# Transposing by the DMA crossbar instead of TensorE: q and the token-mixed rows of batches 1 to 7

## The chip, the cores and the metric

One core of one Trainium2 chip runs the whole program. The metric is the device time of one execution in microseconds, median over several executions. Each run carries the span and the mean clock that the throttle granted to TensorE; a run more than 1.5% above the fastest of the same kernel is called slow, and verdicts use the fast runs alone.

## The reference, cut to what matters

```python
# q, k, v: (8, 8, 576, 64);  out: (8, 576, 512)
k_p, v_p = mean of 8 neighbouring rows of k, v            # 576 -> 72 keys
attn = softmax(q @ k_p.T / 8);  x = attn @ v_p            # heads side by side: (8, 576, 512)
u   = x + (relu(x.T @ w_tok1) @ w_tok2).T                 # token mixing
out = u + relu(u @ w_ch1) @ w_ch2                         # channel MLP, 512 -> 1536 -> 512
```

Two operands must be turned around on the way. The scores need q with the head dimension on the partitions (`qT`), and the channel MLP needs u with the channels on the partitions (`uT`).

## The kernel before

The program is a sequence of *units*. Unit n is the channel MLP of batch n (96 matmuls of 128x512, cut into 48 steps of two), and between its steps stand the pieces of attention and token mixing of batch n+1, at step numbers from a table. TensorE (PE) and GpSimd (POOL) keep the order of the program text.

```python
def load(b):                                   # called in unit n for batch n+2
    kr = raw.tile([SP, H, POOL, D], BF16, name="kr")          # raw: 2 buffers
    vr = raw.tile([SP, H, POOL, D], BF16, name="vr")
    qb = raw.tile([P, HP, BR * D + D], BF16, name="qb")
    nc.vector.memset(qb[:, :, BR * D:], 0.0)                  # zero padding, each batch
    # ... GpSimd issues the casting loads: kr, qb, vr

def qT(hp):                                    # four times for each batch
    def go():
        ps = ps_tr.tile([P, NE, 2, BP], BF16, name="pt")
        for rr in range(NE):
            nc.tensor.transpose(out=ps[:, rr]..., in_=st["qb"][:, hp, rr * P:(rr + 1) * P], identity=ident)
        # copied from PSUM to st["qT"] by ScalarE (VectorE for batch 0)

def uT(c):                                     # four times for each batch, and tails
    def go():
        for kk in range(4):
            nc.tensor.transpose(out=ps[:, kk, :], in_=src[:, kk * P:(kk + 1) * P], identity=ident)
        # copied from PSUM to uT

def unit(n, at):
    if n + 1 < B:
        load(n + 2)
        batches[n + 1][0]()                    # prepare: tiles; GpSimd pools k and v of batch n+1
    for i, _ in enumerate(unit_steps(n, ...)):  # matmuls of the MLP
        # ... the side pieces of step i: kpT, q0.., o/e (scores), av, at, u0.., t0.. (= uT)
```

The softmax here doesn't subtract the row's maximum and nothing guards it: scores larger than these inputs give would overflow.

## Time and profile before

| | before |
|---|---|
| median of the first runs | 307.52 us (307.4 to 308.53) |
| span of the profiled run, mean clock | 305.8 us, 0.996 |
| PE busy | 284.7 us, 93% |
| the first six units, by the start of their first MLP matmul | 34.3, 30.6, 31.9, 30.8, 31.9, 30.8 us |

From the page of the kernel before: the busy time of PE, the clock granted in 40 slices of the span, and the chain of waits that ended last.

```profile
span 305.8 us, 4631 instructions
...
PE 284.7 (93%) x1864; PEld 150.7 (49%) x1900; DVE 157.2 (51%) x316; ACT 102.7 (34%) x181; POOL 135.8 (44%) x120
...
PEclk9999999999999999999999999999999999999998
...
PE 85%; DVE 6%; ACT 3%; DMA 2%; issue 2%; SPq 0%; ACTq 0%
```

PE is the limit. The table by stretches of the same run, one row for a unit, first three units:

```profile
core 0: us, PE busy (x) PEld busy (x) DVE busy (x) ACT busy (x) POOL busy (x), PEclk, DMA share, GB/s
37.18:71.47 34.29, 32.28 (x218) 16.76 (x222) 23.39 (x46) 14.63 (x25) 18.13 (x14) 1.00 0.88 146
71.47:102.08 30.61, 30.15 (x213) 16.43 (x215) 16.81 (x35) 11.15 (x19) 22.29 (x18) 1.00 0.56 92
102.08:133.99 31.91, 31.37 (x218) 17.04 (x222) 17.93 (x37) 11.15 (x19) 19.81 (x15) 1.00 0.54 95
```

The first number after a stretch is its length. PE is idle for about 0.5 us of units 1 and 2. Next, the timeline of PE around one group of q transposes (start, length, line, output and inputs):

```profile
75.09 0.44 PE L217 MATMUL pt<-ident,qb 128*128 128x128 bf16 x5
75.37 0.59 PE L350 MATMUL p_897<-uT,w_ch_86 128*128 128x512 bf16 x2
```

Five transposes are listed with 0.44 us, but the next matmul starts 0.28 us after the first of them; the rest is pipeline. So a group takes 0.28 us of PE's stream. A u group of four takes 0.23 us in the same way.

### The profile page before, as it was taken

The numbers are of one execution on the slowest core, as the hardware profiler recorded it, in microseconds if no ns is written. First come the engines' busy times: TensorE is split into PE (matmuls) and PEld (weight loads), VectorE is DVE, ScalarE is ACT, GpSimd is POOL, SyncE is SP. The second block draws the span as 40 slices with busy tenths as digits, with TensorE's granted clock in tenths as the row PEclk, the third lists the DMA queues.
The fourth block names the chain that finished last, engine by engine and source line by source line (L and its number), as shares of the span: only waits on it lengthen the run. The fifth ranks groups of instructions, "written<-read, shape, count | busy, mean of one in ns | idle before, by whom it ended". The sixth has DMA issues, their size and how long they took to land.

```text
span 305.8 us, 4631 instructions
## 1 busy us (share of the span) xinstructions
PE 284.7 (93%) x1864; PEld 150.7 (49%) x1900; DVE 157.2 (51%) x316; ACT 102.7 (34%) x181; POOL 135.8 (44%) x120
## 2 busy tenths in 40 slices
PE   5687798999999999999999999999999999999993
PEld 2355345445554555445545554455455545444441
DVE  3235657665375537572656266635673567423321
ACT  2154478203810381018301830084008400310300
POOL 8293110996599059913992399995000000000000
PEclk9999999999999999999999999999999999999998
DMA  7999999844772746271836382110121012104023
GB/s 174 194 204 204 203 200 162 140 95 80 119 118 51 141 64 116 52 145 18 140 71 106 58 139 67 46 27 2 34 69 36 0 39 69 36 23 99 16 49 90
DMA packets 26518, 28.27 MB, mean 92 GB/s; under 512 B 4864, under 2 KB 21376, under 8 KB 26496
## 3 DMA queue, kind: packets, MB, share of 16 engines
q0 software_dynamic: 20160, 17.35, 37.0%
q1 hardware_dynamic: 6336, 10.62, 14.1%
q8 instruction: 15, 0.25, 0.3%
q14 instruction: 7, 0.06, 0.1%
HBM read 35.85 MB, written 9.44 MB: 148 GB/s over the span
## 4 chain that ended last, share of the span: by engine, by line
PE 85%; DVE 6%; ACT 3%; DMA 2%; issue 2%; SPq 0%; ACTq 0%
PE pt L217 3%; PE pt L323 3%; DMA qf<-in_q_dram 2%; DVE x L256 1%; DVE kTs_92 L195 1%; PE pt L190 1%; ACT ex L236 1%; DVE kTs_93 L195 1%; PE p_1105 L362 1%; PE p_2921 L362 1%; PE p_3272 L362 1%; PE p_2473 L362 1%; PE p_2878 L362 1%; PE p_1062 L362 1%; PE p_2610 L362 1%
## 5 line engine op out<-in xcount | busy, mean ns | idle before, releaser
L350 PEld LDWEIGHTS <-w_ch_86 128*128 128x128 bf16 x432 | 40.5, 98 | 32.2 <-issue 0.8
L362 PEld LDWEIGHTS <-GT 128*128 128x128 bf16 x432 | 38.7, 98 | 35.9 <-issue 0.5
L104 POOL DMA_DIRECT2D qb<-in_q_dram x7 | 5.4, 777 | 49.9 <-PE pt L217 49.3
L223 ACT COPY qT<-pt 128x640 bf16<-128x640 bf16 x28 | 19.3, 691 | 8.4 <-PE pt L217 7.3
L217 PE MATMUL pt<-ident,qb 128*128 128x128 bf16 x160 | 14.7, 224 | 6.9 <-DVE qT L221 4.7
L246 PEld LDWEIGHTS <-ex 72*128 72x128 bf16 x320 | 15.2, 98 | 11.4 <-DVE x L256 3.3
L217 PEld LDWEIGHTS <-qb 128*128 128x128 bf16 x160 | 11.3, 100 | 17.4 <-issue 10.6
L323 PEld LDWEIGHTS <-u 128*128 128x128 bf16 x128 | 9.7, 98 | 8.6 <-issue 2.0
L325 DVE COPY uT<-pt 128x512 bf16<-128x512 bf16 x28 | 11.8, 421 | 3.5 <-PE pt L323 3.5
L91 POOL DMA_DIRECT2D kr<-in_k_dram x9 | 7.5, 838 | 8.9 <-DVE t_498 L141 8.0
L233 PEld LDWEIGHTS <-kTs_93 128*72 128x72 bf16 x64 | 7.2, 113 | 8.5 <-issue 1.6
L287 PEld LDWEIGHTS <-w_tok_83 128*128 128x128 bf16 x70 | 6.8, 98 | 8.4 <-issue 0.2
L323 PE MATMUL pt<-ident,u 128*128 128x128 bf16 x112 | 10.8, 219 | 0.1
L233 PEld LDWEIGHTS <-kTs_92 128*72 128x72 bf16 x64 | 7.3, 116 | 7.4 <-DVE kTs_92 L195 0.9
L91 POOL DMA_DIRECT2D vr<-in_v_dram x9 | 7.5, 834 | 5.6 <-PE p_396 L390 5.6
L305 PEld LDWEIGHTS <-w_tok_84 128*128 128x128 bf16 x64 | 6.2, 98 | 7.2 <-issue 0.3
L195 DVE COPY kTs_93<-pt 64x576 bf16<-64x576 bf16 (+1 forms) x10 | 4.0, 395 | 4.4 <-PE pt L190 4.3
L190 PEld LDWEIGHTS <-kp 72*128 72x128 bf16 x64 | 3.3, 99 | 4.6 <-DVE kp L208 1.9
L195 DVE COPY kTs_92<-pt 64x576 bf16<-64x576 bf16 (+1 forms) x9 | 3.7, 406 | 3.0 <-PE pt L190 2.0
L190 PE MATMUL pt<-ident,kp 72*128 72x72 bf16 x64 | 3.8, 199 | 1.1 <-DVE kp L208 0.6
L203 PEld LDWEIGHTS <-ident 72*72 72x72 bf16 x32 | 4.3, 135 | 0.7 <-issue 0.2
L355 ACT ACTIVATE GT<-p_3149 128x512 bf16<-128x512 f32 x1 | 0.6, 598 | 11.5 <-PE p_3149 L350 11.5
(806 smaller groups left out, 693.9 us busy)
## 6 DMA issues: line engine op xcount, KB each, us to landing
out_dram<-o SPq DMA_DIRECT2D x72, 128.0 KB, 2.4
kr<-in_k_dram POOLq DMA_DIRECT2D x7, 576.0 KB, 9.7
qb<-in_q_dram POOLq DMA_DIRECT2D x7, 576.0 KB, 6.0
vr<-in_v_dram POOLq DMA_DIRECT2D x7, 576.0 KB, 9.7
w_ch_86<-in_moe_w_ch_dram POOLq DMA_DIRECT2D x3, 512.0 KB, 8.6
w_ch_87<-in_moe_w_ch_dram POOLq DMA_DIRECT2D x3, 512.0 KB, 17.0
qf<-in_q_dram SPq DMA_DIRECT2D x4, 288.0 KB, 4.6
kr<-in_k_dram POOLq DMA_DIRECT2D x2, 288.0 KB, 9.4
```

The lines of the kernel that those rows point to most:

```text
L91: nc.gpsimd.dma_start(out=t[:, h0:h1].rearrange("j h i d -> j h (i d)"), in_=src[b, h0:h1].rearrange("h (j i) d -> j h (i d)", i=POOL))
L190: nc.tensor.transpose(out=ps[:, h, :], in_=st["kp"][:, h].rearrange("j e d -> j (e d)"), identity=ident[0:SP, 0:SP])
L195: copy(out=kT[rows, half, h0 * SP:h1 * SP], in_=ps[rows, h0:h1, :].rearrange("p h j -> p (h j)"))
L217: nc.tensor.transpose(out=ps[:, rr].rearrange("m l p -> m (l p)"), in_=st["qb"][:, hp, rr * P:(rr + 1) * P], identity=ident)
L223: nc.scalar.copy(out=dst, in_=ps)
L233: nc.tensor.matmul(out=ps[0:SP, hl, 0:n], lhsT=kT[:, odd, h * SP:(h + 1) * SP], rhs=st["qT"][:, hp, hl, 0:n], start=True, stop=True)
L246: nc.tensor.matmul(out=ps[:, h // 4, (h % 4) * (D + 1):(h % 4 + 1) * (D + 1)], lhsT=st["ex"][:, h * S + n0:h * S + n0 + P], rhs=st["vp"][: ...
L287: nc.tensor.matmul(out=ps, lhsT=w_tok1[:, CHUNK[c] if c < 4 else 4 + par, m * P:(m + 1) * P], rhs=st["x"][:, c, :] if c < 4 else st["xt"], ...
L323: nc.tensor.transpose(out=ps[:, kk, :], in_=src[:, kk * P:(kk + 1) * P], identity=ident)
L325: copy(out=dst[:, :, o:o + P], in_=ps)
L350: nc.tensor.matmul(out=ps, lhsT=w_ch1[:, kk, m * P:(m + 1) * P], rhs=uT[:, kk, :], start=(kk == 0), stop=(kk == 3))
L362: nc.tensor.matmul(out=ps, lhsT=GT[:, m, c * P:(c + 1) * P], rhs=w_ch2[:, m, :], start=(m == 0), stop=(m == NM - 1))
```

## The change

The intent was to take 268 transposes off the busiest engine, with their PSUM copies, and to give them to the DMA crossbar, which writes SBUF directly. Batch 0 stays on TensorE. The u rows are computed earlier in a unit, to leave the transposes time to land.

```diff
-            st["qT"] = att.tile([P, HP, 2, EV], BF16, name="qT")
+            st["qT"] = att.tile([P, HP, NE, 2, BP], BF16, name="qT")
+            if not first:
+                nc.sync.dma_start_transpose(out=st["qT"].rearrange("m a r l p -> m (a r) (l p)"),
+                                            in_=qb.rearrange("t a e -> t (a e)"))
 ... (score reads the new layout)
@@ def uT(c):
+                if not first:
+                    nc.sync.dma_start_transpose(out=dst[:, :, o:o + P], in_=src)
+                    return
 ...
-    LATER = {1: "kpT", 3: "q0", 5: "q1", 6: "o0", ... 31: "av4", 33: "at0", 34: "at1",
-             37: "u0", 38: "u1", 39: "t0", 40: "u2", 41: "t1", 42: "u3", 43: "u4 t2", 45: "t3", 47: "t4"}
+    LATER = {0: "kpT", 2: "o0", 3: "e0", ... 23: "av4", 26: "at0", 27: "at1", 30: "u0 t0", 31: "u1 t1",
+             32: "u2 t2", 33: "u3 t3", 34: "u4 t4"}
 (FIRST, the table of unit 0, likewise)
```

More of the change, by code (lines that the diff above doesn't have):

```diff
@@ L218, in go @@
                                         in_=st["qb"][:, hp, rr * P:(rr + 1) * P], identity=ident)
-                dst = st["qT"][:, hp].rearrange("m l (r p) -> m r l p", p=BP)
-                if first:
-                    nc.vector.tensor_copy(out=dst, in_=ps)
-                else:
-                    nc.scalar.copy(out=dst, in_=ps)
+                nc.vector.tensor_copy(out=st["qT"][:, hp], in_=ps)
             return go
@@ L233, in go @@
                     nc.tensor.matmul(out=ps[0:SP, hl, 0:n], lhsT=kT[:, odd, h * SP:(h + 1) * SP],
-                                     rhs=st["qT"][:, hp, hl, 0:n], start=True, stop=True)
+                                     rhs=st["qT"][:, hp, 0:n // BP, hl, :], start=True, stop=True)
                 exv = st["ex"][:, 0:H * S].rearrange("j (h n) -> j h n", h=H)
@@ L315, in go @@
                 dst, o = (st["uT"], c * P) if c < 4 else (uT_tails, b // 2 * P)
-                if first:
-                    if c % 2 == 0:
-                        st["uT_ps"] = ps_two.tile([P, 2, 8, P], BF16, name="p2")
-                    ps = st["uT_ps"][:, c % 2, 0:4, :]
-                else:
-                    ps = ps_tr.tile([P, 4, P], BF16, name="pt")
+                if not first:
+                    nc.sync.dma_start_transpose(out=dst[:, :, o:o + P], in_=src)
+                    return
+                if c % 2 == 0:
+                    st["uT_ps"] = ps_two.tile([P, 2, 8, P], BF16, name="p2")
+                ps = st["uT_ps"][:, c % 2, 0:4, :]
                 for kk in range(4):
                     nc.tensor.transpose(out=ps[:, kk, :], in_=src[:, kk * P:(kk + 1) * P], identity=ident)
-                copy = nc.scalar.copy if first and c % 2 == 1 else nc.vector.tensor_copy
+                copy = nc.scalar.copy if c % 2 == 1 else nc.vector.tensor_copy
                 copy(out=dst[:, :, o:o + P], in_=ps)
@@ L376 @@
               av0 av1 d1 av2 at_0 av3 at_2 at_1 av4 d2 at_3 at_4 d2 u0 u1 u2 t0 u3 t1 t2 d1 t3"""
-    FIRST = {8: "K0", 10: "K1", 14: "q0", 15: "kpT0", 17: "q1", 18: "o0", 19: "e0 V0", 20: "kpT1", 21: "o1", 22: "e1 V1",
-             23: "q2", 24: "o2", 25: "e2", 26: "q3", 27: "o3", 28: "e3", 30: "av0", 31: "av1", 32: "av2", 33: "av3",
-             34: "av4", 35: "at0", 36: "at1", 38: "u0", 39: "u1", 40: "t0 u2", 42: "t1 u3", 43: "u4", 44: "t2",
-             46: "t3", 47: "t4"}
-    LATER = {1: "kpT", 3: "q0", 5: "q1", 6: "o0", 7: "q2", 8: "e0", 10: "o1", 11: "q3", 12: "e1", 14: "o2", 16: "e2",
-             18: "o3", 20: "e3", 23: "av0", 25: "av1", 27: "av2", 29: "av3", 31: "av4", 33: "at0", 34: "at1",
-             37: "u0", 38: "u1", 39: "t0", 40: "u2", 41: "t1", 42: "u3", 43: "u4 t2", 45: "t3", 47: "t4"}
+    FIRST = {8: "K0", 10: "K1", 15: "kpT0", 18: "o0", 19: "e0 V0", 20: "kpT1", 21: "o1", 22: "e1 V1",
+             24: "o2 e2", 25: "o3", 26: "e3", 28: "av0", 29: "av1", 30: "av2", 31: "av3", 32: "av4", 33: "at0", 34: "at1",
+             36: "u0 t0", 37: "u1 t1", 38: "u2 t2", 39: "u3 t3", 40: "u4 t4"}
+    LATER = {0: "kpT", 2: "o0", 3: "e0", 5: "o1", 6: "e1", 8: "o2", 9: "e2", 11: "o3", 12: "e3", 15: "av0", 17: "av1",
+             19: "av2", 21: "av3", 23: "av4", 26: "at0", 27: "at1", 30: "u0 t0", 31: "u1 t1", 32: "u2 t2", 33: "u3 t3",
+             34: "u4 t4"}
     warm = singles.tile([P, 512], BF16)
```

## The prediction

> **What bounds the kernel now.** The page's first part has PE busy 284.7 of 305.8 us (93%); the chain of waits is 85% PE. The table by stretches gives the first eight units (a batch's channel MLP with the next batch's attention and token mixing threaded in) 34.3, 30.7, 31.8, 31.0, 32.0, 30.7, 32.6, 20.0 us, PE idle about 0.5 us in each of units 1 to 6. So in units 0 to 6 PE's instruction stream is the time.
>
> **Removed.** 28 groups of five q transposes and 32 groups of four u transposes. The groups table charges 92 to 96 ns each, but that counts the pipeline's overlap. In PE's timeline the next instruction starts 0.28 us after a q group (75.09 to 75.37) and 0.23 us after a u group (65.36 to 65.59): 28 x 0.28 + 32 x 0.23 = 15.2 us of stream. The chain agrees: 3.2% and 2.6% of the span (17.7 us), batch 0's included, which stay. PE's waits on ACT's qT copies (1.4 us) and the single PSUM transpose buffer (1.7 us) mostly go too. ACT's and DVE's copies that go are off the path.
>
> **Added, moved.** Per batch one crossbar transpose of 128x2560 and four or five of 128x512, on SP's queue beside the stores. No trace shows one. The Trainium skill's page "DMA: Bandwidth & Descriptors", section "Latency and other measured facts", gives 261 GB/s: an estimate of 2.5 us for q, 0.5 us for u, plus a fixed part; the trace's 128 KB stores land in 2.4 us. I take 2.5 to 3 us for a u, 5 to 6 us for a q, a new one every 1 to 1.5 us. ("VectorE: DVE Perf Modes", "The three transpose paths", has 1309 ns for one 128x128; as a rate, a u would take 5 us and the change would lose.)
>
> - q: batch 1's qb is issued at 20.5 us and lands 13.1 us later; its first score comes at about 45 us. Later batches have nearly a unit: hidden.
> - u: u3, now at step 33, leaves 14 steps of two matmuls, 6.0 us, before the next unit's first matmul, which needs all four transposes. The DVE add (0.69 us), the queue behind t0 to t2 and the landing take about 6 to 7 us. I charge 0.6 us for each of seven units.
> - kpT at step 0, first score at step 2: two DVE copies (0.92 us) against 0.86 us of matmuls; about 0.3 us a unit, as today at q0.
> - POOL waited 49 us for PE to free qb; it and its loads will run earlier, which should not hold PE.
>
> **Sum.** 307.5 - 15.2 - 3 + 4 + 1 = about 295 us, range 287 to 306. Chances: faster by over 2% 0.74, within 2% 0.18, slower 0.08.
>
> **What would show it.** PE busy falls over 15 us (its groups overlap); units 1 to 6 take 28 to 29.5 us; waits of the first channel matmul on uT by DMA total under 8 us; waits for qT by DMA near zero, except perhaps in unit 0; POOL's wait for qb gone.
>
> **What would make it wrong.** Crossbar transposes of 3 us or more each in series: every unit starts with a wait of 3 us or more, the whole gain. SP's in-order queue holding a transpose behind a store that waits for the unit's last output, or the q transpose issued after those: several us for each batch. Loads sharing the DMA engines. The denser schedule making exp on ACT (0.6 to 0.7 us each) the limit of steps 2 to 12.

## More of the kernel before

The order on VectorE (DVE), ScalarE (ACT) and SyncE (SP) is chosen by a scheduler when the program is built (the instructions of the head and of unit 0 keep their text order on DVE and ACT too, but later ones can be moved in between).

POOL's timeline in unit 1, with the idle time in brackets:

```profile
73.20 0.84 POOL L91 DMA_DIRECT2D kr<-in_k_dram  x1
79.69 0.78 POOL L104 DMA_DIRECT2D qb<-in_q_dram  x1 [5.65 <-PE pt L217]
80.46 0.84 POOL L91 DMA_DIRECT2D vr<-in_v_dram  x1
```

GpSimd waits until PE has transposed the q that still fills the buffer. This wait costs PE nothing, and it puts two of the three loads, and the pooling after them, 8 us and more into unit 1 (71.5 to 102.1).

## The result, and the profile after

| | before | changed |
|---|---|---|
| median (range), 4 runs each | 307.51 us (307.4 to 308.53) | 353.93 us (351.23 to 357.03) |
| span of the profiled run, mean clock | 305.8 us, 0.996 | 350.0 us, 0.923 |
| units 0 to 6 | 34.3, 30.6, 31.9, 30.8, 31.9, 30.8, 31.9 us | 65.2, 43.8, 40.0, 30.3, 29.3, 28.5, 29.3 us |

The changed kernel is slower: the ratio is 1.147 (95% interval 1.136 to 1.158). A ratio here and below is the mean time of one kernel's fast runs over that of the other's fast runs of the same rounds, so it isn't quite the ratio of the medians.

The unit lengths say where to look. Units 4 to 6 are 2.3 to 2.6 us shorter than before, as intended. Units 0 to 2 are longer by 30.9, 13.2 and 8.1 us. The page of the changed kernel:

```profile
span 350.0 us, 4171 instructions
...
PE 282.8 (81%) x1632; PEld 139.4 (40%) x1632; DVE 146.8 (42%) x284; ACT 86.1 (25%) x153; POOL 135.5 (39%) x120
...
PEclk9999965978959989699986999999999999999998
...
PE 64%; DMA 25%; DVE 7%; SPq 1%; issue 1%; ACT 0%; DVEq 0%; ACTq 0%
DMA qT<-qb 13%; DMA uT<-u 9%; DMA qf<-in_q_dram 2%; DVE o L366 1%; PE p_978 L361 1%; DVE x L255 1%; SPq L316 1%; DVE kTs_93 L198 1%; DVE vp L147 1%; PE p_2923 L361 1%; PE p_2329 L361 1%; PE p_2015 L361 1%; PE p_748 L361 1%; PE p_1923 L361 1%; PE p_2580 L361 1%
```

A quarter of the chain is now DMA; 22% of the span are the two new transposes. PE's clock, steady before, drops in the first half. The stretches of units 0, 1, 2 and 5:

```profile
37.00:102.20 65.20, 35.21 (x182) 15.91 (x181) 24.46 (x44) 12.20 (x21) 38.40 (x29) 0.79 1.00 140
102.20:146.00 43.80, 31.58 (x179) 15.34 (x179) 15.14 (x30) 8.79 (x15) 26.78 (x22) 0.89 0.88 132
146.00:186.00 40.00, 31.21 (x182) 15.35 (x183) 16.19 (x32) 8.79 (x15) 19.80 (x15) 0.88 0.64 98
...
245.70:274.20 28.50, 28.35 (x180) 14.43 (x179) 15.10 (x27) 8.79 (x15) 0.00 (x0) 1.00 0.25 55
```

Unit 1 holds 179 matmuls in place of 213, and yet PE is busy for 1.4 us longer: at a clock of 0.89 each takes longer. What PE waited for (total, times, longest):

```profile
PE p_803 L349 <- DMA uT<-u: 11.7, 1, 11.7
PE pt L193 <- DVE kp L144: 11.3, 1, 11.3
PE p_1436 L349 <- DMA uT<-u: 8.2, 1, 8.2
PE p_1115 L349 <- DMA uT<-u: 7.6, 1, 7.6
PE p_668 L245 <- DVE x L255: 5.3, 1, 5.3
```

Two kinds of wait stand here. Three are for `uT`, straight from the DMA, at the start of units 1, 2 and 3. The others are for VectorE. What VectorE itself had waited for:

```profile
DVE qb L84 <- DMA qT<-qb: 28.8, 5, 15.9
```

Line 84 is the zero padding of q's buffer, an instruction of 0.17 us. It may not write before the crossbar has read the buffer's old contents. The scheduler had put it far ahead of where the text has it (the write for batch 5, which the text has in unit 3, stood in unit 0), and in VectorE's in-order stream everything behind it stood still. In VectorE's timeline of unit 0:

```profile
53.93 0.17 DVE L84 MEMSET qb<- 128x128 uint32 x1 [15.90 <-DMA qT<-qb]
54.01 0.62 DVE L142 TENSOR_TENSOR t_489<-t_489 72x512 f32<-72x512 f32 x1
...
70.14 0.20 DVE L250 RECIPROCAL den<-p_640 128x8 f32<-128x8 f32 x1
75.67 0.17 DVE L84 MEMSET qb<- 128x128 uint32 x1 [5.34 <-DMA qT<-qb]
75.76 0.63 DVE L255 TENSOR_TENSOR x<-p_640,den 128x512 bf16<-128x512 f32 x1
```

The wait of 15.9 us fell into the pooling of batch 1's k (L141 to L144), and PE's wait of 11.3 us for `kp` follows from it. In the second place the scaling of x needed only the reciprocal above it, and came 5.4 us after it.

The DMA issues of the page show how long a transpose took from issue to landing, as medians:

```profile
uT<-u SPq DMA_TRANSPOSE x28, 2.8
qT<-qb SPq DMA_TRANSPOSE x7, 7.7
```

The medians hide two groups. The trace's record of each DMA has u mostly at 2.42 to 2.48 us and q at 4.85 us in the later units, where no load runs, but u at 7.7 to 13.5 us in units 0 to 2, and batch 1's q at 22.0 us. The loads now start here (POOL's timeline, end of unit 0):

```profile
83.05 0.84 POOL L91 DMA_DIRECT2D kr<-in_k_dram  x1
83.89 0.78 POOL L104 DMA_DIRECT2D qb<-in_q_dram  x1
84.66 0.84 POOL L91 DMA_DIRECT2D vr<-in_v_dram  x1
```

POOL's wait on PE is gone, as predicted, and the three loads come together. SyncE issued the four u transposes at 84.94, 86.92, 88.56 and 92.37 us. The last load landed at 101.37, the last of the four at 102.11. Batch 1's q was issued at 31.8 us and landed at 53.8; the first of its packets moved at 35.8. What the DMA engines moved while both had work (36 to 52 us; q0 is the loads' queue, q1 SyncE's, with packets, MB and share of the engines' time):

```profile
q0 software_dynamic: 2592, 2.29, 90.5%
q1 hardware_dynamic: 2503, 0.64, 34.5%
...
qT<-qb SPq DMA_TRANSPOSE x1, 22.0
```

And for a q transpose with the engines to itself (224 to 230 us):

```profile
q1 hardware_dynamic: 2592, 0.66, 57.5%
...
qT<-qb SPq DMA_TRANSPOSE x1, 4.8
```

The transpose is 2,592 packets, 2,560 of them of 256 bytes by the trace's packet records; the loads' packets are of 1,024 and 1,152, besides some of 4. Beside each other the two queues moved nearly as many packets (2,503 and 2,592), but bytes 1 to 3.6. The Trainium skill's page "DMA: Bandwidth & Descriptors", section "Queues, rings and completion order", says that a DMA engine goes round its queues packet by packet. This trace agrees, if a turn is one packet as the trace records it (the page counts several descriptors to a packet): with such turns, the queue with the small packets gets the small part of the bytes.

So after the traces there were three suspects. **A**: crossbar transposes crawl while loads are queued. **B**: the padding write blocks VectorE's queue. **C**: SyncE's in-order queue or the new step table is at fault (in the trace SyncE waited 50.4 us in all on `qb` landing before it could issue q transposes, with stores and u transposes behind them).

### The profile page after: what moved, and what is told of

It is laid out like the page before. It is cut to its first block, busy times and chain, and to the rows that moved or that the text cites. A ratio compares the mean times of both kernels' runs of the same rounds, so it can differ in the third digit from the quotient of the medians.

```text
span 350.0 us, 4171 instructions
## 1 busy us (share of the span) xinstructions
PE 282.8 (81%) x1632; PEld 139.4 (40%) x1632; DVE 146.8 (42%) x284; ACT 86.1 (25%) x153; POOL 135.5 (39%) x120
## 4 chain that ended last, share of the span: by engine, by line
PE 64%; DMA 25%; DVE 7%; SPq 1%; issue 1%; ACT 0%; DVEq 0%; ACTq 0%
DMA qT<-qb 13%; DMA uT<-u 9%; DMA qf<-in_q_dram 2%; DVE o L366 1%; PE p_978 L361 1%; DVE x L255 1%; SPq L316 1%; DVE kTs_93 L198 1%; DVE vp L147 1%; PE p_2923 L361 1%; PE p_2329 L361 1%; PE p_2015 L361 1%; PE p_748 L361 1%; PE p_1923 L361 1%; PE p_2580 L361 1%
## 5 line engine op out<-in xcount | busy, mean ns | idle before, releaser
L349 PEld LDWEIGHTS <-w_ch_86 128*128 128x128 bf16 x432 | 41.1, 101 | 63.9 <-issue 32.6
L361 PEld LDWEIGHTS <-GT 128*128 128x128 bf16 x432 | 41.9, 99 | 49.0 <-issue 1.9
L245 PEld LDWEIGHTS <-ex 72*128 72x128 bf16 x320 | 15.2, 99 | 24.1 <-DVE x L255 15.4
L193 PE MATMUL pt<-ident,kp 72*128 72x72 bf16 x64 | 4.8, 226 | 12.0 <-DVE kp L144 11.3
L84 DVE MEMSET qb<- 128x128 uint32 x8 | 1.3, 165 | 28.8 <-DMA qT<-qb 28.8
L349 PE MATMUL p_803<-uT,w_ch_86 128*128 128x512 bf16 x4 | 2.1, 619 | 11.7 <-DMA uT<-u 11.7
L286 PEld LDWEIGHTS <-w_tok_83 128*128 128x128 bf16 x70 | 7.4, 106 | 10.2 <-issue 3.5
L193 PEld LDWEIGHTS <-kp 72*128 72x128 bf16 x64 | 4.1, 118 | 16.4 <-DVE kp L144 11.8
L304 PEld LDWEIGHTS <-w_tok_84 128*128 128x128 bf16 x64 | 6.2, 97 | 7.7 <-issue 0.5
L349 PE MATMUL p_1436<-uT,w_ch_86 128*128 128x512 bf16 x4 | 2.1, 619 | 8.2 <-DMA uT<-u 8.2
L349 PE MATMUL p_1115<-uT,w_ch_86 128*128 128x512 bf16 x4 | 2.1, 617 | 7.6 <-DMA uT<-u 7.6
L144 POOL TENSOR_TENSOR kp<-t_1725 72x512 bf16<-72x512 f32 x1 | 1.3, 1265 | 14.1 <-PE pt L193 14.1
L144 POOL TENSOR_TENSOR kp<-t_2044 72x512 bf16<-72x512 f32 x1 | 1.3, 1258 | 14.1 <-PE pt L193 14.1
L220 PE MATMUL pt<-ident,qb 128*128 128x128 bf16 x20 | 2.3, 262 | 5.3 <-DVE qT L222 4.7
```

Source lines behind the costliest of these rows:

```text
L193: nc.tensor.transpose(out=ps[:, h, :], in_=st["kp"][:, h].rearrange("j e d -> j (e d)"), identity=ident[0:SP, 0:SP])
L245: nc.tensor.matmul(out=ps[:, h // 4, (h % 4) * (D + 1):(h % 4 + 1) * (D + 1)], lhsT=st["ex"][:, h * S + n0:h * S + n0 + P], rhs=st["vp"][: ...
L286: nc.tensor.matmul(out=ps, lhsT=w_tok1[:, CHUNK[c] if c < 4 else 4 + par, m * P:(m + 1) * P], rhs=st["x"][:, c, :] if c < 4 else st["xt"], ...
L304: nc.tensor.matmul(out=ps, lhsT=w, rhs=a, start=(i == 0), stop=(i == len(mms) - 1))
L349: nc.tensor.matmul(out=ps, lhsT=w_ch1[:, kk, m * P:(m + 1) * P], rhs=uT[:, kk, :], start=(kk == 0), stop=(kk == 3))
L361: nc.tensor.matmul(out=ps, lhsT=GT[:, m, c * P:(c + 1) * P], rhs=w_ch2[:, m, :], start=(m == 0), stop=(m == NM - 1))
```

## The experiments

All ran beside runs of the kernel before on the same chip; those had medians of 307.7 to 308.8 us.

### e1_pad_once: padding written once

```diff
-        qb = raw.tile([P, HP, BR * D + D], BF16, name="qb")
-        nc.vector.memset(qb[:, :, BR * D:], 0.0)
+        qb = qbs[b % 2]                        # two lasting tiles
+        if b < 2:
+            nc.vector.memset(qb[:, :, BR * D:], 0.0)
```

> The changed kernel, but with two lasting buffers for q whose zero padding is written once, so VectorE no longer has a write for each batch that waits until the crossbar has read the buffer. Theory A (the crossbar transposes share the DMA engines with the loads and crawl while loads are queued): only VectorE's 28.8 us of waits for qT's transposes go; the waits of the first channel matmul for uT of 7 to 12 us in three units stay, and the first qT still takes about 20 us to land; 335 to 350 us. Theory B (the time is lost in VectorE's in-order queue, the DMA engines being innocent): 315 us or less.

Measured: 346.49, 344.25, 324.71 and 348.55 us. One run in four was much faster, so the others, the profiled one among them, count as slow and there is no ratio. In the profile VectorE waits for no transpose any more, PE waits 37.5 us for uT in three waits, and the first qT takes 23.7 us. It looks as A says, but it decides nothing.

### e2_no_loads: the same, and no loads after batch 1

```diff
+        if b > 1:
+            loaded[b] = kept[b % 2]            # batches 0 and 1 again: wrong result on purpose
+            return
```

> As the run before, and the raw q, k, v of batches 2 to 7 are not loaded: batches 0 and 1's buffers are used again (a wrong result on purpose). SyncE's order of transposes and stores is unchanged. Theory A: from unit 1 on every u transpose lands in about 2.5 us and q in about 5 us, waits for uT under 1 us a unit, units 1 to 6 take 28.5 to 29.5 us each, 292 to 305 us in all, the rest being unit 0, where the weights' loads still run. Theory C (SyncE's in-order queue delays the transposes by itself): waits for uT of several us stay, 320 us or more.

Measured: 294.46 us, ratio 0.954 (0.950 to 0.958). The result is wrong. Units 1 to 6 take 28.5 and 29.4 us in turn, u lands in 2.4 to 2.5 us apart from a few at 3 to 4.2. This is all that PE waited for uT:

```profile
PE p L354 <- DMA uT<-u: 1.5, 1, 1.5
```

SyncE's order of transposes and stores is that of the changed kernel, and so is the step table, which is thereby cleared. SyncE's queue is not yet: without the loads its waits for q's later buffers are gone too. (In e10, below, it waits 100.1 us in all for q's buffers to land, twice as long as in the change, and loses nothing.) With the padding written once, it takes the loads to make the loss; whether the padding writes would cost anything without loads was not run.

### e3_q_only and e4_u_only: one half of the change each

e3 puts u back on TensorE at its old steps, e4 puts q back at steps packed a little closer.

> Only q is transposed by the crossbar; u goes through TensorE at the steps that it had before the change. Theory A with VectorE's wait: the first qT lands after about 20 us and VectorE's padding writes wait, as in the changed kernel, but no wait for uT and less clock lost: 318 to 332 us. If the loss is u's alone: under 302 us.

> Only u is transposed by the crossbar; q goes through TensorE, at steps packed a little closer than before. The loads of q then again wait for TensorE to free the buffer and so start in the first third of a unit. Theory A: u transposes that meet loads land in 5 to 13 us, those that don't in 2.5 us; a wait for uT only where loads overlap; 300 to 318 us. If the loss is q's alone: 300 us or less, with no wait for uT over 1 us.

Measured: e3 330.51 us, ratio 1.071 (1.067 to 1.075). VectorE's padding writes waited 27.7 us for q transposes. e4 311.18 us, ratio 1.005 (0.998 to 1.013), a tie. In e4 GpSimd waits for PE to free q's buffer again, so its q and v loads start 8 us and more into a unit as before; most u transposes meet no load and land in 2.4 to 2.5 us, the worst in 8.1 us, and all waits for uT together are 2.5 us. So u's transposes do not hurt where the loads keep their old place. That e4 gains nothing seems to lie elsewhere (no run isolates it): in its profile, with q packed closer, PE waits 4.0 us for copies of kT (the transposes' one PSUM buffer) and 3.2 us for copies of qT.

### e5_gated_loads and e6_gated_b1_pe: hold the loads back, first try

GpSimd first reads one element of the first relu of unit n, then issues the loads for batch n+2. The pooling of that batch and its q transpose move up into the same unit. e6 puts batch 1's q back on TensorE as well, since it meets the loads of the last weights.

```diff
+            if i == 1 and n + 2 < B:
+                nc.gpsimd.tensor_copy(out=gate[0:1, n:n + 1], in_=gts[-1][0:1, 0, 0:1])
+                load(n + 2)
+                batches[n + 2][0]()            # its tiles, q transpose and pooling
```

> All transposes of the change stay, results are right, q's padding is written once, and GpSimd issues the loads of batch n+2 only after the first relu of unit n (it reads one element of it first), so that they run in the first 16 us of a unit and the u transposes, about 18 us into it, meet no load. Theory A (contention with the loads): u lands in 2.5 to 4.5 us, wait for uT under 1.5 us a unit, units 1 to 6 take 28.5 to 30 us, unit 0 under 38 us, 293 to 302 us: faster than the kernel before. Theory C (SyncE's queue or the step table): 315 us or more.

> As the run before, but batch 1's q, whose crossbar transpose meets the loads of the last weights, goes through TensorE as before the change. Theory A: unit 0 is 34 to 36 us and safe from the weights' loads; 293 to 299 us, within 1.5% of the run before either way, since that one then waits for q's first transpose for 3 us at most.

Measured: 323.82 us, fast and slow runs mixed, and 320.94 us, ratio 1.043. A miss for the time in both, and a hit for the units: units 1 to 6 took 28.5 to 29.4 us in both, with loads running and right results. Unit 0 took 59.6 and 61.3 us. The cause was the experiment's own: VectorE's pooling of batch 1 and GpSimd's pooling of batch 2 took scratch tiles from one ring of two, and in the new order VectorE stood behind GpSimd (a wait of 26.2 us in e5, 24.8 in e6).

### e7_b1_pe: only batch 1's q back on TensorE

> The changed kernel with one thing undone: batch 1's q goes through TensorE. Loads are not held back. Theory A: unit 0, 65 us in the changed kernel, falls to 34 to 42 us; units 1 and 2, where the u transposes still meet loads, stay at 36 to 44 us; 318 to 335 us in all. If the first q transpose were the whole loss: 305 us or less.

Measured: 351.14 us, ratio 1.141 (1.134 to 1.149). A miss: unit 0 fell only to 57.8 us. Padding writes still wait 14.1 us, and u's transposes at the end of unit 0, with loads beside them, took up to 15.0 us. The first q transpose was not the loss; the next ones stepped into its place.

### e8_dose: two loads more, just before the u transposes, in three units

Base e2; two loads of 576 KB into unread tiles at step 24 of units 2, 4 and 6.

> The kernel without the loads of batches 2 to 7 (wrong on purpose, 294.5 us), with two extra loads of 576 KB, of k and of v into buffers that nobody reads, issued at step 24 of units 2, 4 and 6, just before the u transposes. Theory A: there u lands in 5 to 10 us in place of 2.5, the next unit waits 3 to 8 us for it, at half clock for some us after it; units 2, 4 and 6 take 32 to 40 us, the others 28.5 to 29.5; 304 to 325 us. Rival (the loads matter only through the order of waits in the queues): no unit longer by over 1 us.

Measured: 295.43 us, ratio 0.958 (0.950 to 0.967). A miss for the time, a hit for the landing (the profiled run counts as slow, its excess is in unit 0, with 38.9 us): in unit 2 u lands in 7.2, 6.0, 5.2 and 4.2 us, but these loads began 6 us before the first u transpose and were over at 132.8 us; the fourth transpose landed at 134.7, and the next unit was due at just that time. The doses made units 2, 4 and 6 only 0.5 to 0.9 us longer than in e2, which is what the rival had said. But the fourth transpose of unit 2 took 1.8 us longer than in e2, where it had landed 1.8 us before the next unit began: the slack had swallowed the delay. A stretched transpose costs only what exceeds the slack, so this dose was too early to decide; e11 repeats it.

### e9_gated_own_t4 and e10_gated_own_t4_b1_pe: the loads held back, mended

```diff
-        t4 = att.tile([SP, H // 2, 4, D], FP32, name="t4")
+        t4 = att.tile([SP, H // 2, 4, D], FP32, name="t4v" if eng is nc.vector else "t4")
```

> The kernel with held-back loads, mended: VectorE's pooling of batch 1 shared its scratch tile's ring with GpSimd's pooling of batch 2, which the held-back order put ahead of it (VectorE waited 26.2 us, unit 0 took 59.6 us); VectorE now has a ring of its own. Theory A (contention with the loads): units 1 to 6 stay at 28.4 to 29.4 us, unit 0 comes to 34 to 38 us; 293 to 300 us, right results, over 2% faster than the kernel before. If the loss in unit 0 had another cause: unit 0 still over 45 us, 308 us or more.

> As the run before, with batch 1's q through TensorE. Unit 0 34 to 37 us; 292 to 299 us. If q's first crossbar transpose still costs a wait in the run before, this one is 1 to 4 us faster; else the same or 1 us slower.

Measured: e9 294.85, 305.79, 293.65 and 307.30 us, in two groups, so no ratio; its fast profile has units of 33.6, 28.5, 29.3, 28.5, 29.4, 28.5 and 29.3 us. e10 **295.13 us (292.58 to 297.73), ratio 0.947 (0.936 to 0.958), right results**: faster than both kernels (two of its four runs, at 297.1 and 297.7 us, count as slow). From its page:

```profile
PE 272.1 (93%) x1652; PEld 136.5 (47%) x1652; DVE 149.3 (51%) x278; ACT 88.7 (30%) x157; POOL 138.8 (48%) x126
...
uT<-u SPq DMA_TRANSPOSE x28, 2.4
qT<-qbs SPq DMA_TRANSPOSE x6, 6.1
```

And POOL's timeline at the start of its unit 1 (71.3 us): the read of the relu, then the loads.

```profile
73.39 0.18 POOL L407 COPY gate<-GT 1x1 bf16<-1x1 bf16 x1 [6.82 <-ACT GT L361]
73.62 0.89 POOL L94 DMA_DIRECT2D kr<-in_k_dram  x1
74.50 0.78 POOL L107 DMA_DIRECT2D qbs<-in_q_dram  x1
75.27 0.84 POOL L94 DMA_DIRECT2D vr<-in_v_dram  x1
```

The same bytes pass through the same engines; only their time within the unit is another.

### e11_gated_dose: one batch's loads together with the u transposes of one unit

e9, with one more batch's loads in unit 6, issued when u's first row tile is ready, into buffers that are free.

> The mended kernel with one more batch's loads (k, q and v of batch 6 again, into buffers that are free and not read any more, so results stay right), which GpSimd issues in unit 6 when the first row tile of u of that unit is ready, that is together with the u transposes. Theory A: in that unit alone u lands in 9 to 13 us in place of 2.4, all of them about when the loads end, unit 7's first matmul waits 6 to 11 us for uT, the clock halves for some us, and the whole is 7 to 15 us longer than the mended kernel. Rival (not the coincidence with loads but the order of waits in the queues): within 1 us of it.

Measured: 316.58 us, ratio 1.024 (1.015 to 1.033) to the kernel before, which by the 2% rule is unclear; the comparison that matters is by units with e9. Of its profile, the DMA view of the end of unit 6 (247 to 265 us):

```profile
q0 software_dynamic: 2096, 1.77, 69.2%
q1 hardware_dynamic: 3005, 1.14, 48.5%
...
uT<-u SPq DMA_TRANSPOSE x4, 11.1
```

The stretches of units 6 and 7, and PE's waits:

```profile
226.30:264.80 38.50, 29.33 (x183) 14.66 (x183) 16.51 (x29) 8.80 (x15) 2.58 (x4) 0.93 0.64 94
264.80:287.90 23.10, 23.09 (x96) 9.93 (x97) 6.23 (x9) 3.58 (x6) 0.00 (x0) 0.89 0.20 56
```

```profile
PE p L356 <- DMA uT<-u: 11.0, 2, 9.0
PE p L238 <- DMA qT<-qbs: 8.8, 1, 8.8
```

Unit 6 grew from 29.3 to 38.5 us, with a wait of 9.0 us for uT; the u transposes took 8.0, 10.3, 13.8 and 12.0 us and the last two ended at 264.27 and 264.68, with the last load at 264.45. Unit 7 grew from 20.7 to 23.1 us although it waits for nothing new: the clock record is at half for 10.2 us from 259.5 us on. The Trainium skill's page "TensorE: Matmul & The Clock Gate", section "Why this matters for your kernels", warns that an idle gap of over some 3 us drops the clock to half; the trace agrees, with 9.0 us idle. So one batch of badly timed loads costs 11.6 us, 2.4 of it clock. The rest of the difference to e9 is in unit 0 (44.8 us, the wait for qT of 8.8 us), where batch 1's q again met the weights' loads; that is probably e9's slow group too, but no slow run of e9 was profiled.

### e12_gate_alone: loads held back, but padding for every batch

> The changed kernel with the loads held back and VectorE's own scratch ring, but with the zero padding of q written by VectorE for every batch as in the change. Theory A: once loads and transposes keep apart, that write never waits long, so within 1.5% of the mended kernel, 293 to 302 us. If the padding write costs by itself: 305 us or more, with VectorE waiting for qT's transposes.

Measured: 341.6 us, ratio 1.095 (1.080 to 1.109); the profiled run, 342.73 us, counts as slow. A clear miss. I had taken the padding write for a follower of contention. The u transposes land in 2.4 to 4.2 us here and PE waits only 1.5 us for uT, yet VectorE waits 40.9 us in five waits for q's transposes. The scheduler still puts the write early in VectorE's stream, in the middle of a unit whose q transpose is just under way.

### e13_no_gate and e14_pad_each: the best kernel less one mend

> The best kernel (295 us) without its holding back of the loads: padding still written once, batch 1's q still through TensorE. Theory A (contention is a cause of its own): u transposes of units 0 to 2 or 3 land in 8 to 15 us because they meet loads, each of these units is 6 to 12 us longer than in the best kernel, the later ones are 28.5 to 29.4 us; VectorE waits for no transpose; 312 to 335 us. If the padding writes were the only cause: 300 us or less.

> The best kernel with the padding written by VectorE for every batch again, loads held back, batch 1's q through TensorE. Theory: VectorE's in-order queue is a cause of its own: each of four or five units holds one wait of VectorE of 5 to 10 us for a q transpose, during which x and the relus behind it stall TensorE; u transposes all land in 2.4 to 4.5 us with no wait for uT over 2 us; 318 to 338 us. If contention were the only cause: 300 us or less.

Measured: e13 321.73 us, ratio 1.039 (1.031 to 1.047): units 0 to 2 take 36.5, 38.8 and 42.5 us (34.7, 28.5 and 29.4 in e10), u lands in up to 15.2 us in units 1 and 2, VectorE waits for no q transpose. e14 336.93 us, ratio 1.087 (1.077 to 1.098): u lands in 2.4 to 4.4 us. The two profiles' waits, PE's in e13 and VectorE's in e14:

```profile
PE p L351 <- DMA uT<-u: 23.9, 3, 11.9
```

```profile
DVE qb L85 <- DMA qT<-qb: 37.0, 4, 15.9
```

Both times were as expected, except that e13's unit 0 is only 1.8 us longer, where 6 to 12 had been expected: its four u transposes met no load and landed in 2.4 to 3.4 us. The two causes are separate: each alone keeps the kernel slower than before. From the change to the best kernel, one mend added at a time:

| kernel | median us | ratio to before |
|---|---|---|
| the change | 353.93 | 1.147 |
| + batch 1's q on TensorE (e7) | 351.14 | 1.141 |
| + padding written once (e13) | 321.73 | 1.039 |
| + loads held back, own scratch ring (e10) | 295.13 | 0.947 |

The rows come from different rounds. In this order the padding writes are worth 29 us and holding the loads back 27 us (30 and 28 by the fast runs alone). In another order the shares differ (e1, padding first, gained less in most runs), since each stall moves the loads and transposes of the next unit.

## Why the prediction was wrong

It said 295 us, 287 to 306; the measured median was 353.93 us.

- **What leaves PE: right.** 15.2 us of stream were predicted. Units 4 to 6 of the changed kernel are 2.3 to 2.6 us shorter, and in the kernels without stalls units 1 to 6 take 28.5 to 29.4 us, where "28 to 29.5" was predicted. e10 is 13.6 us under the median of before of its rounds. PE's busy time fell less than the "over 15 us": by 12.6 us in e10 (which keeps batch 1's q on TensorE), and by 1.9 us in the change, whose matmuls ran partly at half clock.
- **The transpose by itself: right.** "2.5 to 3 us for a u, 5 to 6 us for a q, a new one every 1 to 1.5 us": 2.44 and 4.85 us, one u every 1.3 us, when nothing else used the DMA engines.
- **"I charge 0.6 us for each of seven units": the term that was mis-sized.** It priced a transpose on idle DMA engines. Beside loads u took 7.7 to 13.5 us, and three waits for uT came to 27.5 us in place of 4.
- **"POOL waited 49 us for PE to free qb; it and its loads will run earlier, which should not hold PE": the step that failed.** That wait had kept two of each unit's three loads at its first third. Without it the three loads fell upon the u transposes (84.66 and 84.94 us), whose landing PE waits for. e11 shows this coincidence as a cause: 11.6 us for one batch's loads. Contention was named among what would make the prediction wrong, but not carried into the sum.
- **"Later batches have nearly a unit: hidden", and batch 1's first score "at about 45 us": wrong, and for another reason too.** Batch 1's q took 22.0 us beside the loads of weights and of the next batch, in place of 5 to 6, and landed at 53.8 us. Beyond that, the score's inputs were looked at, but not who else waits for a q transpose. The padding write inherits the wait for the buffer's reader. When that reader was PE, it seldom held VectorE (2.0 us in one wait in before's tile view of qb); with the crossbar as reader it waited 28.8 us and carried pooling, softmax scaling and relus with it. The prediction has no term for it; e14 shows that it costs 42 us over e10 by itself, in a kernel with the loads held back.
- **The clock** was no term either. It was 0.996 before and 0.923 after, since each of PE's six waits of over 4 us after the head has a stretch at half clock, which begins in the wait or within 0.3 us of its end.
- **Still open.** SyncE's order was never varied alone. It is harmless where loads and transposes keep apart (e10, with 100.1 us of SyncE's waits for q's buffers), but how much the q transposes waiting at its head added in unit 0 of the changed kernel no run isolates. Nor was the small difference of e7 to the change split further, and no run put the padding write later in VectorE's order instead of writing it once.

## What to carry to other kernels

When a wait disappears, ask what it had been scheduling: here a stall that cost nothing kept the loads away from the only stretch in which their bandwidth was later needed. A DMA on the critical path must be priced together with whatever shares the engines at that moment, above all if its packets are smaller than its neighbours'. And when an operation changes engine, list every instruction that waits for it to *read* its input, not only those that want its output: a cheap write in an in-order queue can stop everything behind it.

## What the Trainium skill lacked or had wrong

- "DMA: Bandwidth & Descriptors", "Rules for kernel authors", says that "A transpose next to ordinary DMAs needs nothing". The row is about results, and these were indeed right in every run meant to be right. In time it is not so: u took 2.44 us alone and up to 15.2 us beside loads (e13), q 4.85 and 22.0 us. No page says how small a share of the bytes a transpose gets beside loads: here 0.64 of 2.92 MB in 16 us.
- "Advanced Engine Details and Errata", "X-Bar Transpose (TRN2)", says that transposing DMAs are as fast as regular ones. Alone that holds (u 2.44 us, a store of as many bytes 2.2 to 2.5 us, but for two). Beside loads it does not: two stores at 83.7 and 84.3 us took 6.1 and 6.8 us, the three u transposes issued next 10.9, 13.5 and 13.0 us.
- "VectorE: DVE Perf Modes", "The three transpose paths", gives 1309 ns for one 128x128 by the crossbar without saying that this is no rate: four of them landed in 2.44 us, twenty in 4.85 us.
- "DMA: Bandwidth & Descriptors", "Latency and other measured facts", gives 261 GB/s, measured on one kernel with a non-contiguous middle dimension; here the packets of a lone q transpose, 655 KB, ran for 3.23 us (225.91 to 229.13 us), which is 203 GB/s.
- No page gives the time for which a transposing DMA of such a size holds the engine that issues it: SyncE 1.22 us for a u and 3.06 us for a q alone, up to 10.8 us for a q beside loads (e1).
